# Pooled attention feeding a max-out MLP, one core: the last pair's x transposed on TensorE, a corrected model in the instruction planner, and a new rank between two kinds of jobs

## The chip, the cores and the metric

The kernel runs on one core of a Trainium2 chip. The metric is the device time of one execution, in microseconds (us), as the median of several executions. TensorE (PE in the profile) multiplies matrices into PSUM, ScalarE (ACT) does the exponentials, VectorE (DVE) moves results out of PSUM, GpSimd (POOL) casts inputs to bf16, and the queue of SyncE (SP) starts nearly all transfers. PEld is TensorE's loading of weights, which the profile lists on its own.

## The reference

Shapes: q, k, v are 8 batches x 8 heads x 1152 x 64; w1 and w2 are 512 x 1024; w_out is 1024 x 512.

```python
q_pool = q.reshape(B, H, S // 2, 2, D).mean(axis=3)      # 576 queries
attn = softmax(q_pool @ k.T / sqrt(D))
x = (attn @ v)  ->  [B * 576, H * D] = [4608, 512]
out = maximum(x @ w1, x @ w2) @ w_out
```

The kernel writes the maximum as `x @ w2 + relu(x @ (w1 - w2))`. With `wd = w1 - w2` and `w21 = w2 @ w_out`, the output is `x @ w21 + relu(x @ wd) @ w_out`.

## The kernel before

Two heads of a batch make a **pair**; there are 32 pairs, four to a batch. For each pair POOL casts q (adding the two pooled rows), k and v to bf16; q and k are brought into transposed form (`qpT`, `kT`), on TensorE for the first pairs and by a transposing DMA for the later ones. The scores of a pair form one long strip of 9 x 576 columns, cut into **groups** of 512 (324 in all). A group is two row tiles, one for each head: 64 rows of the array each, working at the same time (`scores`, L533). ACT takes the exponential of a group in one instruction (L540) into `et`. A group is written into one of three PSUM buffers `sps`, or of two after group `NARROW` (45), when the third is given to the other jobs.

All other TensorE work is a **job** of one kind, with its PSUM bank or banks and an evacuation:

- q and k: transposes for the next pairs (L410, L438).
- a: the product of `et` with `vE`, two jobs for a pair, each five chunks of nine matmuls (L384), then a reciprocal and a multiplication on DVE (L471, L473) into `xnat`.
- x: `xnat` of a pair transposed to `xT`, features by tokens. Batches 0 and 7 (`X_PE`) do this on TensorE in `xtrans_pe`: five transposes over the whole array (L589) into one bank and one DVE copy (L594). Batches 1 to 6 do it in `xtrans` by one transposing DMA for each pair (L575), issued by SP.
- w: the preparation of `w2T` and `w21`.
- h: a relu job, four matmuls over the features of up to 384 tokens with `wd`, evacuated through a relu into the ring `gT` (L686 on DVE, L682 on ACT in the tail). It needs `xT` of all four pairs of the batch.
- p: an output job of 128 tokens, four matmuls of `xT` with `w21` and eight of `gT` with `wo`, copied out (L715, L712) and stored (L662).

Full-array work is mode "f", work in two row tiles is mode "s". Between `NARROW` and the last group two h jobs or two p jobs run as a `Pair` in mode "s": a matmul of one job in the low rows beside one of the other in the high rows, in two banks.

**What sets the order.** No order is written by hand. The class `Plan` holds a model: a time at which each engine is free, a cost for each instruction, a latency after it, and one clock for all transfers, `dma_free`. `op` records an instruction at its modelled time. The loop at the end of the kernel asks at each step what TensorE could begin now by that model (a group of scores, or the next unit of a running job, by `rank`), and records it. `flush` issues loads, casts, transposing DMAs and stores when the model says that they are due; a load goes out only while `dma_free` is less than `DEPTH` = 4 us ahead. The recorded order is then emitted, with semaphores, as a fixed program for each engine. So each engine works through a fixed list: where an instruction's input is later than the model thought, all that stands behind it on its engine is late too.

`refill` gives free banks to jobs, in the order q, k, x, a, then w, p, h; a Pair needs two free banks, and no more than two Pairs run at a time (one while "a" jobs wait). Among running jobs `rank` decides: q and k 6, x 5, a 4, w 3, p 2, h 1.

Of the kernel before, what the change touches and what calls it, by code (L numbers as in the profile page):

```python
# [7 lines left out]
P = 128  # L8
# [7 lines left out]
class Plan:  # L16
# [11 lines left out]
    def __init__(self):  # L28
        self.ops = []
        self.writer = {}  # L30
        self.readers = {}
        self.free = {}
        self.dma_free = 0.0
        self.mode = None
        self.last = {}
        self.issued = 0
        self.pages = {}
# [19 lines left out]
    def fetch(self, t, n):  # L57
# [7 lines left out]
                t = max(t, self.pages[k])  # L65
        return t

    def op(self, eng, fn, r=(), w=(), dma=None, cost=0.1, mode="f", after=(), solo=False, done=None, n=0):
        me = len(self.ops)
        assert all(k in self.writer for k in r), r  # L70
        deps, raw = self.deps(r, w, after)
        if done is not None:
            deps.add(done)
        prev = self.last.get(eng)
        if prev is not None and (solo or self.ops[prev]["solo"]):
            deps.add(prev)
            raw.add(prev)
        self.last[eng] = me
        t = self.when(eng, r, w, after)
        if done is not None:  # L80
            t = max(t, self.ops[done]["seen"] + 0.05)
        if dma is not None:
            self.free[eng] = t + (1.3 if mode == "t" else 0.5)
            self.dma_free = max(self.free[eng] + 1.2, self.dma_free) + cost
            seen = self.dma_free + 0.7
        else:
            if eng == "PE" and mode != self.mode:
                t += 0.1
                self.mode = mode
            if eng == "PE":  # L90
                t = self.fetch(t, n)
            self.free[eng] = t + cost
            seen = t + cost + self.LAT[eng]
        self.ops.append(dict(eng=eng, fn=fn, deps=deps, raw=raw, dma=dma, w=tuple(w),
                             seen=seen, end=self.free[eng], solo=solo, done=done, mode=mode, cost=cost))
        for k in r:
            self.readers.setdefault(k, set()).add(me)
        for k in w:
            self.writer[k] = me
            self.readers[k] = set()  # L100
        return me
# [63 lines left out]
class Job:  # L165


    def __init__(self, kind, units, evac, done=None, nb=None, split=False):
        self.kind, self.units, self.evac, self.done = kind, units, evac, done
        self.nb, self.split = nb, split  # L170


# [16 lines left out]
class Pair:  # L189


    def __init__(self, one, two):
        self.kind, self.jobs = one.kind, (one, two)
# [12 lines left out]


def bass_funnel_attn__then__act_maxout2_kernel(
# [32 lines left out]
    with ctx:  # L241
# [138 lines left out]
        def plan_unit(u, ms, gate):  # L380

            def whole(e):
                for at, lhs, rhs, start, stop in u.parts:
                    last = e.matmul(fb[ms[0]][:, at:at + rhs.shape[-1]], lhs, rhs, start=start, stop=stop)  # L384
                return last

            def crossed(e):
                for p, q, phase, first, fin in u.parts:
                    for half, (at, lhs, rhs, *_), m in ((0, p, ms[phase]), (1, q, ms[1 - phase])):
                        last = e.matmul(fb[m][:, at:at + rhs.shape[-1]], lhs[rows(half)], rhs[rows(half)],  # L390
                                        start=first, stop=fin)
                return last

            if u.go is not None:
                fn = lambda e: u.go(e, ms[0])
# [5 lines left out]
        def dve(fn, r, w, cost):  # L401
            op("DVE", fn, r=r, w=w, cost=cost)

        def qtrans(i, lo=0, hi=QU, tag="", key=None):
            s = i % 2

            def go(e, m):
                mb = fb[m][:, :].bitcast(BF16)
                for u in range(lo, hi):
                    last = e.transpose(  # L410
                        mb[:, u * HP:(u + 1) * HP],
                        qp[s][:, u, :, :].rearrange("p h d -> p (h d)"), ident[0:HP, 0:HP])
                return last

            def evac(m):
                mb = fb[m][:, :].bitcast(BF16)
                dve(lambda e: e.tensor_copy(qpT[i % 3][:, lo * HP:hi * HP], mb[:, lo * HP:hi * HP]),
                    [f"f{m}"], [key or f"qpT{i % 3}", f"f{m}"] + (["qpT0.0"] if i == 3 else []),
                    0.06 + 0.038 * (hi - lo))
# [10 lines left out]
        def ktrans_pe(i, cuts=(0, 5, 9)):  # L430
# [3 lines left out]
            for lo, hi in zip(cuts, cuts[1:]):  # L434
# [8 lines left out]
                def evac(m, lo=lo, hi=hi):  # L443
                    mb = fb[m][:, :].bitcast(BF16)
                    dve(lambda e: e.tensor_copy(
                        kT[v3][:, lo:hi, :].rearrange("p t x -> p (t x)"),
                        mb[:, 0:(hi - lo) * P]),
                        [f"f{m}"], kkeys(i, lo, hi) + [f"f{m}"], 0.1 + (hi - lo) * 0.12)
# [133 lines left out]
        def xtrans_pe(i):  # L582
# [9 lines left out]
            def evac(m):  # L592
# [4 lines left out]
            return Job("x", [unit([f"xn{xs}.{2 * pr + half}" for half in range(2)] + ["ident"], 0.28, go)],  # L597
                       evac)

        def xkeys(n0, n1, cts):  # L600
            return [f"xT.{j}.{ct}" for j in range(n0 // HP, n1 // HP) for ct in cts]

# [8 lines left out]
        def w_cast(part, ct):  # L611
            if part == 0:
                dve(lambda e: e.tensor_copy(w2b[:, ct, :], w2f[:, ct, :]),
                    [f"w2f{ct}"], [f"w2b{ct}"], 0.6)
            elif part == 1:
                assert f"w2T{ct}" in plan.writer
                dve(lambda e: e.tensor_tensor(  # L617
                    wd[:, ct, :], w1f[:, ct, :], w2f[:, ct, :], ALU.subtract),
                    [f"w1f{ct}", f"w2f{ct}"], [f"wd{ct}", f"w2b{ct}", "w2f"], 1.2)
            else:  # L620
                dve(lambda e: e.tensor_copy(
                    wo[:, 2 * ct:2 * ct + 2, :], wof[:, 2 * ct:2 * ct + 2, :]),
                    [f"wof{ct}"], [f"wo{2 * ct}", f"wo{2 * ct + 1}"], 0.6)

        def w2t_job(ct):
            def go(e, m):
# [6 lines left out]
            def evac(m):  # L633
                mb = fb[m][:, :].bitcast(BF16)
                dve(lambda e: e.tensor_copy(
                    w2T[:, ct, :, :].rearrange("p f x -> p (f x)"), mb[:, 0:F]),
                    [f"f{m}"], [f"w2T{ct}", "w2T", f"f{m}"], 1.15)
            return Job("w", [unit([f"w2b{ct}", "ident"], 0.44, go)], evac)

        def w21_jobs():  # L640
# [178 lines left out]
        def flush():  # L819
# [22 lines left out]
                if plan.ops[plan.writer[f"osb{o}"]]["seen"] + 2.0 <= now():  # L842
                    store(*held.pop(o))
            for i in list(x_wait):
                if i // NHP in X_PE:
                    x_wait.remove(i)
                    queue["x"].append(xtrans_pe(i))
                elif plan.ops[plan.writer[f"xn{i // NHP % 2}.{2 * (i % NHP) + 1}"]]["seen"] <= now():
                    x_wait.remove(i)
                    xtrans(i)  # L850
# [54 lines left out]
        def refill():  # L905
# [2 lines left out]
            tail = nxt == NGR  # L908
            soon = now() + 0.05
            spare.sort(key=bank_at)  # L910
            pairs = sum(isinstance(r.job, Pair) for r in running)
            kinds = [r.job.kind for r in running]
            for kind in "qkxa" + ("wh" if queue["a"] and "p" in kinds else "wph"):
                while queue[kind] and spare and bank_at(spare[0]) <= now() + (9.0 if tail else 0.3):
                    wide = NARROW <= nxt < NGR and queue[kind][0].split
                    if wide and (len(spare) < 2 or pairs >= (1 if queue["a"] else 2)):
                        break
                    if wide and kind == "p" and "p" in kinds:
# [51 lines left out]
        def emit_unit(run):  # L970
# [4 lines left out]
                return  # L975
            running.remove(run)
            spare.extend(run.ms)
            for j, m in zip(job.jobs if isinstance(job, Pair) else (job,), run.ms):
                j.evac(m)
                finish(j)  # L980

        def finish(job):
# [58 lines left out]
        load("q", 4, load_q, "qraw1")  # L1041
        load("v", 3, load_v, "vraw0")
        start_w(1)
        rank = {"q": 6, "k": 6, "x": 5, "a": 4, "w": 3, "p": 2, "h": 1}
        while p_end[0] < NTOK:
            flush()
            refill()
# [91 lines left out]
```

## Time and profile before

| what | us |
|---|---|
| median of 3 executions | 384.81 (384.6 to 388.63) |
| the profiled execution, whole | 385.84 |
| its span, first to last instruction | 384.1 |
| PE busy | 362.5 (94%) |
| ACT busy | 316.9 (83%) |
| POOL busy | 162.1 (42%) |
| DVE busy | 140.6 (37%) |

The times of the table are of one profiled execution, apart from the first row. Busy time of PE is that of matmuls, which are pipelined and overlap, so a busy PE isn't one without gaps; the idle time before PEld shows gaps of some tenths of a microsecond that PE's row hides. In a row of the timeline stand the start, the duration, the engine, the line, the operation, what it writes and reads, the count, and in brackets the idle time before it with what ended it. A row of the groups has busy time and the mean of one in ns behind the bar.

### The profile page before, as it was taken

To read this page: it belongs to the slowest core of one execution; us is meant where nothing else is said; L and a number is where in the kernel's file an instruction comes from. 1 tells how busy PE (TensorE), PEld (TensorE's weight loads), DVE (VectorE), ACT (ScalarE), POOL (GpSimd) and SP (SyncE) were. 2 spreads that over 40 slices of the span, in tenths; PEclk is the share of its full clock that TensorE was granted. 3 is DMA by queue.
4 is the path that set the end of the run, shared out by engine and by line. 5 is a ranking of instruction groups with operands and counts; after the bars stand their busy time and mean duration, and the time that the engine had idled before them with its cause. 6 is when DMAs were issued, how large, how long until landed. Compare 5 with 4: busy or idle time off the path is not lost.

```text
span 384.1 us, 13179 instructions
## 1 busy us (share of the span) xinstructions
PE 362.5 (94%) x5928; PEld 232.9 (61%) x5936; DVE 140.6 (37%) x322; ACT 316.9 (83%) x358; POOL 162.1 (42%) x135
## 2 busy tenths in 40 slices
PE   4889989999599999999899999999999999999996
PEld 2456556666276666666575666666666666664754
DVE  3267943523132332512442413252324244351321
ACT  5998989899769999899889999999899998961320
POOL 2856587665433553634455365364454401000000
PEclk9898999999989999999999999999999999999999
DMA  8999999999997999999999899999999750203223
GB/s 281 409 390 401 361 270 318 223 340 294 266 343 228 212 268 234 272 255 241 277 262 239 267 264 285 229 272 267 248 274 205 129 111 6 56 3 82 58 55 82
DMA packets 95160, 89.09 MB, mean 232 GB/s; under 512 B 67456, under 2 KB 68224, under 8 KB 95104
## 3 DMA queue, kind: packets, MB, share of 16 engines
q1 hardware_dynamic: 94672, 87.86, 89.3%
q8 instruction: 46, 0.75, 0.8%
q10 hardware_dynamic: 432, 0.39, 0.4%
q14 instruction: 10, 0.08, 0.1%
HBM read 62.91 MB, written 9.44 MB: 188 GB/s over the span
## 4 chain that ended last, share of the span: by engine, by line
PE 79%; DMA 9%; ACT 6%; DVE 3%; SPq 1%; issue 1%; POOL 1%
PE sps L384 20%; PE sps L533 17%; PE fb L390 16%; PE fb L384 14%; PE sps L390 10%; ACT et L540 6%; DMA qraw<-in_q_dram 4%; DMA xT<-xnat 3%; DVE wd L617 1%; DMA kraw<-in_k_dram 1%; SPq L662 1%; POOL qp L353 1%; DVE xnat L473 1%; PE fb L589 0%; DVE stage L686 0%
## 5 line engine op out<-in xcount | busy, mean ns | idle before, releaser
L540 ACT ACTIVATE et<-sps 128x1024 bf16<-128x1024 f32 (+1 forms) x336 | 306.1, 1010 | 29.9 <-PE sps L533 27.7
L533 PE MATMUL sps<-qpT,kT 64*128 64x256 bf16 (+7 forms) x1162 | 121.4, 290 | 4.5 <-ACT et L540 2.8
L353 POOL TENSOR_TENSOR qp<-qraw 64x576 bf16<-64x576 f32 x62 | 87.7, 1414 | 14.1 <-DMA qraw<-in_q_dram 7.4
L367 POOL TENSOR_SCALAR vE<-vraw 128x1152 bf16<-128x1152 f32 x32 | 38.1, 1190 | 127.8 <-PE sps L384 84.4
L533 PEld LDWEIGHTS sps<-qpT,kT 64*128 64x128 bf16 x1162 | 46.9, 95 | 53.0 <-ACT et L540 26.9
L384 PEld LDWEIGHTS sps<-vE,et 128*128 128x128 bf16 x1530 | 49.3, 98 | 9.4 <-issue 4.4
L384 PE MATMUL sps<-vE,et 128*128 128x65 bf16 x1530 | 53.8, 194 | 0.0
L384 PEld LDWEIGHTS fb<-vE,et 128*128 128x128 bf16 x1350 | 43.7, 98 | 10.1 <-issue 4.1
L384 PE MATMUL fb<-vE,et 128*128 128x65 bf16 x1350 | 48.1, 194 | 0.8 <-DVE w L648 0.8
L329 POOL TENSOR_SCALAR kbf<-kraw 128x1152 bf16<-128x1152 f32 x31 | 36.4, 1173 | 13.4 <-DMA kraw<-in_k_dram 11.2
L686 DVE TENSOR_SCALAR stage<-sps 128x384 bf16<-128x384 f32 (+1 forms) x67 | 28.0, 452 | 36.6 <-PE sps L390 27.0
L390 PE MATMUL sps<-xT,wd 64*128 64x384 bf16 (+1 forms) x448 | 40.8, 286 | 0.2
L390 PE MATMUL fb<-xT,wd 64*128 64x384 bf16 (+1 forms) x384 | 35.0, 287 | 5.8 <-DMA xT<-xnat 5.4
L390 PE MATMUL fb<-wo,stage 64*128 64x512 bf16 x288 | 39.9, 376 | 0.0
L471 DVE RECIPROCAL rc<-sps 128x5 f32<-128x5 f32 x34 | 6.6, 195 | 65.8 <-PE sps L384 65.8
L686 DVE TENSOR_SCALAR stage<-fb 128x384 bf16<-128x384 f32 (+1 forms) x48 | 20.1, 461 | 24.0 <-PE fb L390 23.9
L390 PEld LDWEIGHTS fb<-xT,wd 64*128 64x128 bf16 x384 | 16.4, 94 | 15.5 <-DMA xT<-xnat 5.9
L390 PEld LDWEIGHTS sps<-xT,wd 64*128 64x128 bf16 x448 | 19.3, 94 | 9.9 <-DVE stage L715 0.6
L715 DVE COPY stage<-fb 128x512 f32<-128x512 f32 x19 | 12.3, 687 | 29.0 <-PE fb L390 24.4
L471 DVE RECIPROCAL rc<-fb 128x5 f32<-128x5 f32 x30 | 5.8, 195 | 42.3 <-PE fb L384 42.3
L390 PE MATMUL fb<-w,xT 64*128 64x512 bf16 x144 | 21.0, 376 | 0.1
L390 PEld LDWEIGHTS fb<-wo,stage 64*128 64x128 bf16 x288 | 13.4, 94 | 9.4
(59 smaller groups left out, 221.7 us busy)
## 6 DMA issues: line engine op xcount, KB each, us to landing
vraw<-in_v_dram SPq DMA_DIRECT2D x32, 576.0 KB, 7.1
kraw<-in_k_dram SPq DMA_DIRECT2D x31, 576.0 KB, 6.1
qraw<-in_q_dram SPq DMA_DIRECT2D x31, 576.0 KB, 5.2
out_dram<-stage SPq DMA_DIRECT2D x70, 128.0 KB, 3.9
xT<-in_moe_w_dram SPq DMA_DIRECT2D x4, 512.0 KB, 11.6
stage<-in_moe_w_out_dram SPq DMA_DIRECT2D x4, 512.0 KB, 15.1
stage<-in_moe_w_dram SPq DMA_DIRECT2D x4, 512.0 KB, 12.9
kT<-kbf SPq DMA_TRANSPOSE x27, 4.8
```

The costliest lines, as they stand in the source:

```text
L329: op("POOL", lambda g: g.tensor_scalar(kbf[s][:, :, :, :].rearrange("p t h d -> p h t d"), kraw[r][:, :, :, :], 1.0, 1.0, ALU.mult, ALU.mu ...
L353: op("POOL", lambda g, half=half, a=a: g.tensor_tensor(qp[s][:, :, half, :], a[:, :, 0, :], a[:, :, 1, :], ALU.add), r=[f"qraw{r}"], w=[f" ...
L367: op("POOL", lambda g: g.tensor_scalar(vE[r][:, :, :, 0:D].rearrange("p t h d -> p h t d"), vraw[r][:, :, :, :], 1.0, 1.0, ALU.mult, ALU.m ...
L384: last = e.matmul(fb[ms[0]][:, at:at + rhs.shape[-1]], lhs, rhs, start=start, stop=stop)
L390: last = e.matmul(fb[m][:, at:at + rhs.shape[-1]], lhs[rows(half)], rhs[rows(half)], start=first, stop=fin)
L471: dve(lambda e: e.reciprocal(rc[half][:, :], a[:, :, 64:65]), [f"f{m}"], [f"rc{half}"], 0.19)
L473: dve(lambda e: e.tensor_tensor(xnat[xs][:, i % NHP, :, half * D:half * D + D], a[:, :, 0:D], rc[half][:, :].unsqueeze(2).to_broadcast([P, ...
L533: last = e.matmul(sps[r][:, h, col:col + hi - lo], kT[i % 3][rows(h), t, :], qpT[i % 3][rows(h), lo:hi], start=True, stop=True)
L540: op("ACT", lambda e: e.activation(et2[:, :, c:c + z - a], sps[r][:, :, a - g * W:z - g * W], EXP, scale=scale), r=[f"s{r}"], w=keys + [f" ...
L617: dve(lambda e: e.tensor_tensor(wd[:, ct, :], w1f[:, ct, :], w2f[:, ct, :], ALU.subtract), [f"w1f{ct}", f"w2f{ct}"], [f"wd{ct}", f"w2b{ct} ...
L686: dve(lambda e: e.tensor_scalar_max(gT[:, ft, g0:g0 + size], fb[m][:, 0:size], 0.0), [f"f{m}"], w, 0.1 + size / 960.0)
L715: dve(lambda e: e.tensor_copy(osb[o][:, 0:n], fb[m][:, 0:n]), [f"f{m}"], [f"osb{o}", f"f{m}"], 0.1 + n / 966.0)
```

## The change

1. **x of the last pair of each batch.** In `flush`, pairs whose number within the batch is 3 go to TensorE in all batches, so those of batches 1 to 6 no longer use the transposing DMA. While `NARROW <= nxt < NGR` the new `xtrans_two` is used for every x job on TensorE: nine transposes of 64 rows by 128 columns, in the two row tiles (mode "s"), five of the low rows into one bank and four of the high rows into another, and three DVE copies in place of one. Such a job is `two`: it needs two banks and counts as a Pair.
2. **The planner's model.** SP and ACT are first free at 0.75 us; a plain transfer after a transposing one costs 0.65 more; a transfer is seen 0.8 us (a transposing one 1.2) after its end, where it was 0.7; several DVE costs change; VectorE's large casts of weights (mode "b") and POOL's work slow one another (`share`).
3. **Rank.** h has rank 2 and p has rank 1.

```diff
-        self.free = {}
+        self.free = {"SP": 0.75, "ACT": 0.75}
+        self.turned = False
...
+    def share(self, other, t, cost):
+
+        last = self.last.get(other)
+        if last is None or other == "DVE" and self.ops[last]["mode"] != "b":
+            return 0.0
+        both = 0.8 * max(0.0, min(cost, self.free[other] - t))
+        self.free[other] += both
+        self.ops[last]["seen"] += both
+        return both
...
             self.free[eng] = t + (1.3 if mode == "t" else 0.5)
+            if self.turned and mode != "t":
+                self.dma_free += 0.65
+            self.turned = mode == "t"
             self.dma_free = max(self.free[eng] + 1.2, self.dma_free) + cost
-            seen = self.dma_free + 0.7
+            seen = self.dma_free + (1.2 if mode == "t" else 0.8)
...
+            if eng == "POOL" or mode == "b":
+                cost += self.share("DVE" if eng == "POOL" else "POOL", t, cost)
...
-                    0.06 + 0.038 * (hi - lo))
+                    0.12 + 0.038 * (hi - lo))
...
-                        [f"f{m}"], kkeys(i, lo, hi) + [f"f{m}"], 0.1 + (hi - lo) * 0.12)
+                        [f"f{m}"], kkeys(i, lo, hi) + [f"f{m}"], 0.13 + (hi - lo) * 0.072)
...
+        def xtrans_two(i):
+            b, pr = i // NHP, i % NHP
+            xs, n0 = b % 2, b * SQ
+
+            def go(e, *ms):
+                for j in range(NCH + 1):
+                    for half, m in zip(range(2 if j < NCH else 1), ms):
+                        mb = fb[m][:, :].bitcast(BF16)
+                        last = e.transpose(mb[:, j * HP:(j + 1) * HP], xnat[xs][rows(half), pr, j, :],
+                                           ident[rows(half), rows(half)])
+                return last
+
+            def evac(*ms):
+                for half, m in enumerate(ms):
+                    n = NCH + 1 - half
+                    mb = fb[m][:, :].bitcast(BF16)[:, 0:n * HP].rearrange("p (j x) -> p j x", x=HP)
+                    to = xT[:, pr, n0 + half * HP:n0 + half * HP + NCH * P].rearrange(
+                        "p (j x) -> p j x", x=P)[:, :, 0:HP]
+                    parts = [(to, mb[:, 0:NCH, :], 0.3)]
+                    if half == 0:
+                        parts.append((xT[:, pr, n0 + NCH * P:n0 + SQ], mb[:, NCH, :], 0.13))
...
+            return Job("x", [unit([f"xn{xs}.{2 * pr + half}" for half in range(2)] + ["ident"],
+                                  0.19, go, "s")], evac, two=True)
...
-                    [f"w2f{ct}"], [f"w2b{ct}"], 0.6)
+                    [f"w2f{ct}"], [f"w2b{ct}"], 0.65, "b")
...
-                    [f"w1f{ct}", f"w2f{ct}"], [f"wd{ct}", f"w2b{ct}", "w2f"], 1.2)
+                    [f"w1f{ct}", f"w2f{ct}"], [f"wd{ct}", f"w2b{ct}", "w2f"], 1.2, "b")
...
-                    [f"f{m}"], [f"w2T{ct}", "w2T", f"f{m}"], 1.15)
+                    [f"f{m}"], [f"w2T{ct}", "w2T", f"f{m}"], 0.68)
...
-                if i // NHP in X_PE:
+                if i // NHP in X_PE or i % NHP == NHP - 1:
                     x_wait.remove(i)
-                    queue["x"].append(xtrans_pe(i))
+                    queue["x"].append((xtrans_two if NARROW <= nxt < NGR else xtrans_pe)(i))
...
-            pairs = sum(isinstance(r.job, Pair) for r in running)
+            pairs = sum(len(r.ms) > 1 for r in running)
...
-                    wide = NARROW <= nxt < NGR and queue[kind][0].split
+                    wide = queue[kind][0].two or NARROW <= nxt < NGR and queue[kind][0].split
...
-        rank = {"q": 6, "k": 6, "x": 5, "a": 4, "w": 3, "p": 2, "h": 1}
+        rank = {"q": 6, "k": 6, "x": 5, "a": 4, "w": 3, "p": 1, "h": 2}
```

More of the change, by code (lines that the diff above doesn't have):

```diff
@@ L165, with __init__ @@
 class Job:
-    def __init__(self, kind, units, evac, done=None, nb=None, split=False):
+    def __init__(self, kind, units, evac, done=None, nb=None, split=False, two=False):
         self.kind, self.units, self.evac, self.done = kind, units, evac, done
+        self.two = two
         self.nb, self.split = nb, split
@@ L192, in __init__ @@
     def __init__(self, one, two):
-        self.kind, self.jobs = one.kind, (one, two)
+        self.kind, self.jobs, self.two = one.kind, (one, two), False
         self.units = []
@@ L394, in plan_unit @@
             if u.go is not None:
-                fn = lambda e: u.go(e, ms[0])
+                fn = lambda e: u.go(e, *ms)
             else:
@@ L399, in plan_unit, with dve @@
                n=2 * len(ms) * len(u.parts) if u.parts else 2 * u.many)
-        def dve(fn, r, w, cost):
-            op("DVE", fn, r=r, w=w, cost=cost)
+        def dve(fn, r, w, cost, mode="f"):
+            op("DVE", fn, r=r, w=w, cost=cost, mode=mode)
         def qtrans(i, lo=0, hi=QU, tag="", key=None):
@@ L598, in xtrans_pe @@
                        evac)
+        def xtrans_two(i):
[17 more added lines that the diff above has]
+                        parts.append((xT[:, pr, n0 + NCH * P:n0 + SQ], mb[:, NCH, :], 0.13))
+                    for k, (to, a, cost) in enumerate(parts):
+                        op("DVE", lambda e, to=to, a=a: e.tensor_copy(to, a), r=[f"f{m}"],
+                           w=([f"xT.{(n0 + half * HP) // HP + 2 * j}.{pr}" for j in range(NCH)] if k == 0 else
+                              [f"xT.{(n0 + SQ) // HP - 1}.{pr}"]) + ([f"f{m}"] if k == len(parts) - 1 else []),
+                           after=under(n0, n0 + SQ) + [f"spill{pr}"], cost=cost)
+            return Job("x", [unit([f"xn{xs}.{2 * pr + half}" for half in range(2)] + ["ident"],
+                                  0.19, go, "s")], evac, two=True)
         def xkeys(n0, n1, cts):
@@ L622, in w_cast @@
                     wo[:, 2 * ct:2 * ct + 2, :], wof[:, 2 * ct:2 * ct + 2, :]),
-                    [f"wof{ct}"], [f"wo{2 * ct}", f"wo{2 * ct + 1}"], 0.6)
+                    [f"wof{ct}"], [f"wo{2 * ct}", f"wo{2 * ct + 1}"], 0.65, "b")
         def w2t_job(ct):
@@ L977, in emit_unit @@
             spare.extend(run.ms)
-            for j, m in zip(job.jobs if isinstance(job, Pair) else (job,), run.ms):
-                j.evac(m)
+            pair = isinstance(job, Pair)
+            for j, ms in zip(job.jobs, [[m] for m in run.ms]) if pair else [(job, run.ms)]:
+                j.evac(*ms)
                 finish(j)
```

## The prediction

> **What bounds the kernel now.** The page comes first, for the balance of the engines; then the table by stage; then the list of waits of TensorE; then the timeline around the two places that this list points to.
>
> ```profile
> span 384.1 us, 13179 instructions
> PE 362.5 (94%) x5928; PEld 232.9 (61%) x5936; DVE 140.6 (37%) x322; ACT 316.9 (83%) x358; POOL 162.1 (42%) x135
> ```
>
> TensorE is busy 94% of the span and ACT 83%. An average over stages says little, so here is the table by stage: the stretch and its length, then busy time (and instructions) of PE, PEld, DVE, ACT and POOL, then the granted clock, the share of the DMA engines and GB/s.
>
> ```profile
> 10.00:60.00 50.00, 44.77 (x714) 28.38 (x716) 28.44 (x51) 46.09 (x52) 34.68 (x26) 0.93 1.08 366
> 60.00:335.00 275.00, 267.81 (x4765) 173.92 (x4760) 95.19 (x234) 250.27 (x276) 125.03 (x99) 0.99 0.99 237
> 341.00:384.10 43.10, 39.60 (x324) 24.24 (x325) 10.58 (x23) 9.32 (x21) 0.00 (x0) 0.99 0.29 62
> ```
>
> From 60 to 335 us PE is idle for only 7.2 us of 275 and ACT for 24.7. After 341 us the scores are over, ACT is nearly done, and TensorE alone works for 43 us through relu and output jobs left over. So **the sum of TensorE's work and gaps sets the end**: a microsecond of TensorE won in the score stage lets relu and output work move out of the tail. What waits does PE have?
>
> ```profile
> PE fb L390 <- DMA xT<-xnat: 5.4, 2, 4.0
> PE fb L410 <- DVE qp L361: 4.8, 1, 4.8
> PE sps L533 <- ACT et L540: 2.8, 8, 0.6
> PE fb L410 <- POOL qp L353: 0.9, 1, 0.9
> PE fb L384 <- DVE w L648: 0.8, 1, 0.8
> ```
>
> The columns are total, times, longest. The 4.8 is one wait, for the cast of the first pair's q. The largest other item is two waits, of 4.0 and so 1.4 us, of relu jobs for x that a transposing DMA brings. The longer one:
>
> ```profile
> 95.16 3.14 SPq L662 DMA_DIRECT2D out_dram<-stage  x4
> 98.34 0.59 SPq L309 DMA_DIRECT2D qraw<-in_q_dram  x1
> 99.40 0.38 SPq L301 DMA_DIRECT2D kraw<-in_k_dram  x1
> 99.83 1.25 SPq L575 DMA_TRANSPOSE xT<-xnat  x1
> 105.91 0.82 PE L390 MATMUL fb<-xT,wd 64*128 64x192 bf16 x10 [4.02 <-DMA xT<-xnat]
> 107.00 1.02 ACT L540 ACTIVATE et<-sps 128x1024 bf16<-128x1024 f32 x1 [3.80 <-PE sps L533]
> ```
>
> The x of pair 7, the last of batch 1, stands on SP's queue behind four stores and two loads, is issued at 99.83 and lands some 6 us later. The planner had put relu matmuls that need it ahead of the next scores, so PE stops from 101.9 to 105.9, and ACT with it. The other wait is for the last pair of batch 3:
>
> ```profile
> 182.84 1.28 SPq L575 DMA_TRANSPOSE xT<-xnat  x1
> 190.19 0.26 PE L390 MATMUL fb<-xT,wd 64*128 64x192 bf16 x2 [1.43 <-DMA xT<-xnat]
> ```
>
> And the first gap is not over when it ends:
>
> ```profile
> 102.00:106.00 4.00, 0.09 (x2) 0.09 (x2) 0.72 (x2) 1.20 (x2) 0.00 (x0) 1.00 1.06 287
> 106.00:108.00 2.00, 1.94 (x37) 1.56 (x38) 0.62 (x2) 1.00 (x1) 0.00 (x0) 0.77 1.16 311
> 108.00:110.00 2.00, 2.00 (x32) 1.68 (x31) 0.51 (x2) 0.02 (x1) 0.00 (x0) 0.50 1.12 395
> 110.00:112.00 2.00, 2.00 (x51) 1.60 (x49) 0.22 (x2) 1.94 (x2) 0.00 (x0) 0.88 1.00 368
> 186.00:190.00 4.00, 2.69 (x52) 1.61 (x46) 1.87 (x6) 3.86 (x5) 1.29 (x2) 1.00 1.03 264
> ```
>
> After it the clock is 0.77, 0.50 and 0.88 in three stretches of 2 us, which loses 0.46 + 1.0 + 0.24 = **1.7 us**. After the short wait the clock stays at 1.00.
>
> **The change, part by part.** *The two waits go.* Both are for a last pair's x; the change takes all six such transposes off the DMA queue. Nothing on TensorE then waits for SP at a batch's end: -5.4 us of idle and -1.7 us of cold clock. What is late next is the product of the last pair itself, through DVE's normalisation, the transposes and DVE's copies, all of which the planner orders with durations it knows.
>
> *What TensorE takes on.* Nine transposes in 64 rows, six times. No row has them in two tiles; the nearest has nine in one tile, and the whole-array form has five:
>
> ```profile
> 12.68 0.33 PEld L410 LDWEIGHTS fb<-ident,qp 64*128 64x128 bf16 x9
> 337.75 0.38 PE L533 MATMUL sps<-qpT,kT 64*128 64x320 bf16 x4
> 338.06 0.28 PEld L589 LDWEIGHTS sps<-ident,xnat 128*128 128x128 bf16 x5 [0.21 <-issue]
> 338.44 0.11 PEld L390 LDWEIGHTS fb<-xT,wd 64*128 64x128 bf16 x4
> 338.55 0.46 DVE L594 COPY xT<-sps 128x576 bf16<-128x576 bf16 x1 [0.45 <-PE sps L589]
> ```
>
> The nine take 0.33 us in one tile. Two tiles at the same time could halve that to 0.17; at the pace of the whole-array form they would take 0.28 x 9 / 5 = 0.50. I take 0.33, the row of the same shape: 6 x 0.33 = **+2.0 us**, with 1.0 and 3.0 as ends.
>
> *Four transposes change form*: those of pair 3 and of the first three pairs of batch 7, which now are whole-array work between work in row tiles. In the fence above such a job costs 0.21 idle before, 0.28, and 0.10 to the next load (338.34 to 338.44): 0.59. In row tiles there is no change of mode: 0.33. So 4 x 0.26 = **-1.0 us**.
>
> *DVE.* Three copies of 256, 64 and 256 columns take the place of one of 576 (four times) or of none (six times).
>
> ```profile
> L594 DVE COPY xT<-fb 128x576 bf16<-128x576 bf16 x7 | 3.2, 456 | 1.6 <-PE fb L589 1.6
> L417 DVE COPY qpT<-fb 128x256 bf16<-128x256 bf16 x1 | 0.3, 291 | 0.5 <-PE fb L410 0.5
> ```
>
> At 0.29 for each of the large ones and at most that for the small one, 0.87 us a time; 10 x 0.87 - 4 x 0.46 = 6.9 us more on DVE, which from 60 to 335 us is busy for 95 of 275. Other evacuations have room around it, so I count nothing. Without that cover, the relu work of a batch would begin 0.4 us later, six times 0.4: 2.5 us.
>
> *SP and DMA.*
>
> ```profile
> xT<-xnat SPq DMA_TRANSPOSE x24, 6.0
> ```
>
> Six of these 24 issues, of 1.25 us each, leave SP's queue, and six transposes the DMA engines, whose share is 0.99 over the score stage. That can only bring other transfers forward; SP doesn't set the end, so nothing is counted.
>
> *The planner's model.* It computes nothing and adds no instruction; it re-orders. Three of the new costs can be set against rows:
>
> ```profile
> L445 DVE COPY kT<-fb 128x640 bf16<-128x640 bf16 x5 | 2.5, 492 | 5.7 <-PE fb L438 5.7
> L635 DVE COPY xT<-fb 128x1024 bf16<-128x1024 bf16 x4 | 2.7, 686 | 0.6 <-PE fb L629 0.4
> L617 DVE TENSOR_TENSOR wd<-stage,xT 128x1024 bf16<-128x1024 f32 x4 | 6.9, 1735 | 0.0
> ```
>
> The copy of five k blocks was modelled at 0.70 and is now at 0.49 (measured 0.492); that of `w2T` at 1.15, now 0.68 (0.686); the subtraction of weights at 1.2, now 1.2 plus what POOL costs it (1.735). So the model comes nearer to this trace. What that is worth can't be summed: the fixed order of some 13,000 instructions is drawn anew. Upper bound of the gain: PE's idle time between 10 and 60 us is 5.2 us, of which the rows above name 0.9 and 0.8 behind POOL and DVE. Upper bound of the loss: a wait like the present one, 5.7 us with its cold clock, at a new place. I take 0 and keep -3 and +6.
>
> *Rank.* Relu jobs go first among those running, and output jobs fill in. The work is the same; in the tail PE is busy 39.6 of 43.1 us in either order, about 3 us of the rest being the last copies and stores. I take 0.
>
> **The sum.** 385.84 (this execution) - 5.4 - 1.7 + 2.0 - 1.0 = 379.7 us. The profiled execution is 1.0 above the median of the runs shown (384.81), so by that median: **378.7 us**, 1.6% less. A change under 1% is about what a measurement of this kernel can't tell from none; that is 381.0 to 388.7.
>
> **Rivals.**
>
> *More is won* (0.08): the corrected model also closes gaps of 10 to 60 us, where the clock is 0.93 on the mean (3.5 us lost) and PE is idle for 5.2. Half of both is 4.3: 374.4. Against it: those gaps go with loads, k casts and ACT's pace, which the new numbers don't change.
>
> *The new order brings its own wait* (0.25): one gap of the present kind, 5.7 us, anywhere in the score stage, cancels the gain: 384.4. For it: the planner's order has 324 groups and over 100 jobs, and two misjudged transfers cost 7 us before; 18 transposing DMAs for x stay. Against it: those are for earlier pairs, which relu work doesn't need at once.
>
> *Banks* (0.10, slower). `xtrans_two` needs two banks and counts as a Pair, of which two may run. In the score stage four banks serve all jobs. An output Pair has now the lowest rank and keeps its two banks while relu Pairs pass; the x job then waits for a relu Pair to finish, its matmuls and two evacuations by L686:
>
> ```profile
> L686 DVE TENSOR_SCALAR stage<-fb 128x384 bf16<-128x384 f32 x26 | 13.3, 553 | 14.1 <-PE fb L390 14.1
> ```
>
> That is two times 0.55 plus about 0.9 us of matmuls, 2 us, and the "a" jobs queue for the same banks. If each of the ten x jobs delays the chain by 1 us on x and 0.2 on the product after it, 12 us come on top: 390.7. It decides from the point where PE has no other work ready while x waits; against it stands that a relu Pair or the output Pair itself is then there to run.
>
> *Loads are held back* (0.05, slower). Per pair the model's transfers sum to 8.5 us (k, q, v 4.45; transposes 3.15; stores 0.9); with 0.65 for one or two turns 9.2 to 9.8, close to the 10.4 us that a pair has (the scores end at about 341 us and begin at 7, for 32 pairs). With `DEPTH` a load then goes out later, casts and transposing DMAs follow, and ACT starves: 0.4 us a pair for 28 pairs, 389.9. It decides if the modelled sum passes the pair's time.
>
> *A cold clock from transposes* (0.02). The first two rows below show q transposes and behind them a clock of 0.57; if each of the six new jobs did that, at 1.7 us each, 378.7 + 10.2 = 388.9. Against it stands the x job on TensorE at 338.06 us, and the third row:
>
> ```profile
> 27.72 0.42 PE L410 MATMUL fb<-ident,qp 64*128 64x64 bf16 x9 [0.87 <-POOL qp L353]
> 28.00:32.00 4.00, 4.00 (x56) 2.70 (x54) 2.65 (x5) 3.30 (x4) 0.39 (x1) 0.57 1.05 398
> 336.00:344.00 8.00, 7.78 (x134) 4.93 (x132) 3.92 (x9) 6.51 (x8) 0.00 (x0) 1.00 0.01 2
> ```
>
> The clock is 1.00 around it. The Trainium skill, "TensorE: Matmul & The Clock Gate", section "Part 4: PE-mode transpose", says that transposes don't count as busy for the clock in the way that matmuls do, which speaks for this rival. By that rule the time would be its 388.9. With some 0.3 us of transposes among dense matmuls the trace doesn't bear it out.
>
> **How the numbers follow.** Forecast 0.50, with its own range 375.5 to 381.0 from the ends of the priced terms and a small loss or gain in the order; more won 0.08; own wait 0.25; banks 0.10, held loads 0.05 and cold clock 0.02 together 0.17. So faster 0.58, same 0.25, slower 0.17. The range from 374 to 389 leaves out about 0.05 below and 0.15 above.
>
> **What would show it.** Right: 18 DMA transposes of x; no wait of PE for x by DMA at a batch's end; clock 1.00 in every slice of the score stage; six more x jobs, of about 0.33 us of PEld, with no idle time before them from a change of mode; the tail shorter or the scores over earlier. Wrong: waits of PE or PEld for DVE's x copies, for banks, or for another DMA of several tenths at each batch; a new gap of microseconds; ACT waiting for scores for more than 27.7 us in all, the present sum:
>
> ```profile
> ACT et L540 <- PE sps L533: 27.7, 39, 3.8
> ```

## The result, and the profile after

The changed kernel takes 375.11 us (374.37 to 375.7), the kernel before beside it 386.01: a ratio of 0.971, 95% interval 0.965 to 0.977. The forecast was 378.7, within 374 to 389. The sign and the wide range held; the time lies 0.4 us below the forecast's own range, 375.5 to 381.0. The gain is 10.9 us where 6.1 were forecast, so nearly half of it has another source than the sum names. The profiled execution takes 375.68 us.

The page of the kernel after, its span and engines, and then the table by stage with the stretches that were read before (busy time and instructions of PE, PEld, DVE, ACT and POOL, then clock, DMA share, GB/s):

```profile
span 373.9 us, 13143 instructions
PE 358.2 (96%) x5910; PEld 231.7 (62%) x5910; DVE 142.6 (38%) x337; ACT 316.8 (85%) x361; POOL 163.7 (44%) x135
```

```profile
10.00:60.00 50.00, 46.90 (x789) 30.13 (x788) 28.86 (x56) 48.21 (x55) 36.22 (x26) 0.97 1.10 360
60.00:335.00 275.00, 271.09 (x4834) 176.36 (x4831) 100.59 (x250) 254.86 (x280) 125.35 (x99) 1.00 0.98 235
341.00:373.90 32.90, 29.82 (x190) 17.07 (x188) 6.05 (x13) 6.11 (x15) 0.00 (x0) 1.00 0.38 80
```

PE's idle time from 60 to 335 us falls from 7.2 to 3.9 us, its clock there is 1.00, and what is left after 341 us is 10.2 us shorter. The waits of PE and of ACT (total, times, longest), and the transposing transfers of x:

```profile
PE fb L427 <- DVE qp L378: 4.8, 1, 4.8
PE sps L550 <- ACT et L557: 2.7, 8, 0.6
PE sps L401 <- issue: 1.1, 2, 0.6
```

```profile
ACT et L557 <- PE sps L550: 18.1, 34, 1.0
```

```profile
xT<-xnat SPq DMA_TRANSPOSE x18, 6.3
```

No wait of PE for x by DMA is left, and ACT's wait for scores has gone from 27.7 to 18.1 us. The new x job, for the last pair of batch 1, in the timeline after:

```profile
92.93 0.49 DVE L490 TENSOR_TENSOR xnat<-sps,rc 128x320 bf16<-128x320 f32 x1
...
93.47 0.40 PEld L625 LDWEIGHTS sps<-ident,xnat 64*128 64x128 bf16 x9
93.69 0.30 PE L625 MATMUL sps<-ident,xnat 64*128 64x64 bf16 x9
94.03 0.58 DVE L639 COPY xT<-sps 128x256 bf16<-128x256 bf16 x3 [0.61 <-PE sps L625]
...
95.46 0.49 PE L407 MATMUL sps<-xT,wd 64*128 64x192 bf16 x8
```

DVE's normalisation ends at 93.42, the copies of x at 94.61, and the job's own loads of weights don't wait. Before, the same x was issued at 99.83 and landed at about 105.9.

*Where the time went.* ACT's busy time up to a moment is a measure of how far the scores have come. The same three stretches, first of the kernel before, then after:

```profile
0.00:60.00 60.00, 49.17 (x749) 30.95 (x754) 31.68 (x59) 51.38 (x57) 37.11 (x37) 0.94 1.03 352
60.00:110.00 50.00, 45.31 (x801) 29.96 (x797) 16.81 (x42) 41.20 (x45) 26.49 (x21) 0.97 1.15 291
110.00:320.00 210.00, 207.50 (x3706) 134.44 (x3704) 73.55 (x182) 195.34 (x216) 98.54 (x78) 1.00 1.01 239
```

```profile
0.00:60.00 60.00, 51.29 (x825) 32.63 (x826) 32.10 (x64) 53.48 (x60) 38.34 (x37) 0.97 1.06 347
60.00:110.00 50.00, 47.69 (x899) 32.41 (x896) 18.31 (x49) 45.58 (x51) 30.17 (x24) 1.00 1.09 275
110.00:320.00 210.00, 209.00 (x3653) 133.88 (x3651) 76.71 (x184) 197.94 (x219) 95.18 (x76) 1.00 1.01 239
```

After 60 us ACT is 2.1 us ahead, in the next 50 us it gains 4.4 more (the long wait was there), from 110 to 320 another 2.6. The last exponential of the scores and what follows it:

```profile
334.59 7.61 ACT L540 ACTIVATE et<-sps 128x1024 bf16<-128x1024 f32 x8 [0.47 <-PE sps L533]
```

```profile
327.26 4.70 ACT L557 ACTIVATE et<-sps 128x1024 bf16<-128x1024 f32 x5
```

These are before and after: the scores end at 342.2 and at 332.0. What comes behind them is 41.9 us long in both (384.1 - 342.2 and 373.9 - 332.0). So the whole gain of 10.2 us lies ahead of the last exponential, and **the tail did not grow** although the scores were done 10 us sooner.

### The profile page after: what moved, and what is told of

Read it like the earlier page. It is cut to its first block, busy times and chain, and to the rows that moved or that the text cites. A ratio compares the mean times of both kernels' runs of the same rounds, so it can differ in the third digit from the quotient of the medians.

```text
span 373.9 us, 13143 instructions
## 1 busy us (share of the span) xinstructions
PE 358.2 (96%) x5910; PEld 231.7 (62%) x5910; DVE 142.6 (38%) x337; ACT 316.8 (85%) x361; POOL 163.7 (44%) x135
## 4 chain that ended last, share of the span: by engine, by line
PE 78%; ACT 19%; DMA 1%; DVE 1%; issue 1%
PE sps L401 20%; ACT et L557 19%; PE sps L550 17%; PE fb L401 15%; PE fb L407 12%; PE sps L407 12%; DMA qraw<-in_q_dram 1%; DVE stage L761 0%; PE fb L455 0%; PE fb L427 0%; DVE kT L462 0%; DVE qp L378 0%; ACT stage L758 0%; PE sps L625 0%; PE fb L625 0%
## 5 line engine op out<-in xcount | busy, mean ns | idle before, releaser
L557 ACT ACTIVATE et<-sps 128x1024 bf16<-128x1024 f32 (+1 forms) x336 | 305.7, 1014 | 20.1 <-PE sps L550 18.1
L401 PEld LDWEIGHTS fb<-vE,et 128*128 128x128 bf16 x1485 | 47.6, 97 | 11.2 <-issue 4.8
L401 PE MATMUL fb<-vE,et 128*128 128x65 bf16 x1485 | 52.6, 193 | 0.0
L401 PEld LDWEIGHTS sps<-vE,et 128*128 128x128 bf16 x1395 | 44.2, 97 | 10.1 <-issue 5.3
L401 PE MATMUL sps<-vE,et 128*128 128x65 bf16 x1395 | 48.6, 193 | 1.1 <-issue 1.1
L732 DVE TENSOR_SCALAR stage<-sps 128x384 bf16<-128x384 f32 (+3 forms) x65 | 30.1, 496 | 50.6 <-PE sps L407 42.0
L407 PE MATMUL sps<-xT,wd 64*128 64x384 bf16 (+1 forms) x416 | 44.1, 313 | 0.0
L407 PE MATMUL fb<-xT,wd 64*128 64x384 bf16 (+1 forms) x288 | 28.6, 301 | 0.4 <-DVE stage L761 0.4
L732 DVE TENSOR_SCALAR stage<-fb 128x384 bf16<-128x384 f32 (+2 forms) x39 | 17.4, 484 | 27.8 <-PE fb L407 25.4
L407 PE MATMUL sps<-wo,stage 64*128 64x512 bf16 x160 | 23.4, 376 | 0.0
L490 DVE TENSOR_TENSOR xnat<-fb,rc 128x320 bf16<-128x320 f32 x33 | 16.2, 491 | 1.1
```

The costliest lines, as they stand in the source:

```text
L490: dve(lambda e: e.tensor_tensor(xnat[xs][:, i % NHP, :, half * D:half * D + D], a[:, :, 0:D], rc[half][:, :].unsqueeze(2).to_broadcast([P, ...
L557: op("ACT", lambda e: e.activation(et2[:, :, c:c + z - a], sps[r][:, :, a - g * W:z - g * W], EXP, scale=scale), r=[f"s{r}"], w=keys + [f" ...
L732: dve(lambda e: e.tensor_scalar_max(gT[:, ft, g0:g0 + size], fb[m][:, 0:size], 0.0), [f"f{m}"], w, 0.1 + size / 960.0)
```

## The experiments

The change has three parts: X (x of the last pairs), M (the planner's numbers), R (the rank). The six combinations other than the two kernels themselves were run, then variants. In the expectations, "exponential 48" is the start time of the 49th exponential, which the trace gives as 54.6 us before and 50.4 after.

**One part alone, and X taken out.**

```diff
 e1_x_only: before, with xtrans_two and
+                if i // NHP in X_PE or i % NHP == NHP - 1:
 e2_model_only: before, with the new costs, share, turned, seen and first free times
 e3_rank_only: before, with
+        rank = {"q": 6, "k": 6, "x": 5, "a": 4, "w": 3, "p": 1, "h": 2}
 e4_no_x: after, with
-                if i // NHP in X_PE or i % NHP == NHP - 1:
+                if i // NHP in X_PE:
```

> Only the x of each batch's last pair goes to TensorE, in two row tiles; the planner's numbers and the rank are those of before. Theory A (the two waits for x by DMA are most of the gain): the two waits of 4.0 and 1.4 us and the cold clock after the first go, the first 40 us stay as before, 378 to 380 us. Theory B (the corrected model is most of it): 383 to 386. Theory C (each edit draws a new order and the gains don't add): anywhere, with a new wait of 2 us or more of TensorE somewhere in the score stage.

> Only the planner's numbers are changed; x stays on the transposing DMA, the rank as before. Theory A: the first 60 us gain about 2 us (exponential 48 at 50.4 us in place of 54.6), one or two waits for x by DMA of 1 us or more stay, 382 to 385 us. Theory B: 377 or less. Theory C: anywhere.

> Only the ranks of relu and output jobs are exchanged. Theories A and B: within 1.5 us of before, 385 to 387, with the waits for x by DMA still there. A theory that the rank wins: 382 or less, with less idle time of ACT in the score stage. Theory C: anywhere, more than 2 us from before.

> The changed kernel with x back on the transposing DMA: model and rank new. Theory A: the waits for x by DMA come back, 380 to 384 us. Theory B: 375 to 377, as the changed kernel. Theory C: anywhere between 375 and 388.

| kernel | parts | median us (range) | ratio to before, 95% interval |
|---|---|---|---|
| e1_x_only | X | 380.63 (379.81 to 383.63) | 0.989 (0.984 to 0.995) |
| e2_model_only | M | 378.98 (378.37 to 379.94) | 0.983 (0.979 to 0.988) |
| e3_rank_only | R | 384.71 (382.86 to 386.52) | 0.998 (0.996 to 1.001) |
| e4_no_x | M, R | 377.47 (377.14 to 378.29) | 0.980 (0.976 to 0.984) |
| e5_no_rank | X, M | 380.04 (379.09 to 381.08) | 0.984 (0.978 to 0.991) |
| e6_no_model | X, R | 379.25 (379.01 to 379.49) | 0.982 (0.976 to 0.988) |
| after | X, M, R | 375.11 (374.37 to 375.7) | 0.971 (0.965 to 0.977) |

X alone brings 1.1%, M alone 1.7%, R alone nothing that can be measured. Theory A (X is most of it) and theory B (M is) both fall: either brings most of the same thing, and e4, which A put at 380 to 384 us with the waits back, takes 377.47 without them. Theory C holds in that the gains don't add; the new wait of 2 us or more that it names for e1 is in none of the six. But each kernel is one order drawn by the planner, and no run draws another order with the same parts, so a difference of 1 or 2 us between two kernels can be the draw rather than the part. In e1 and e2 alike PE has no wait for x by DMA. The kernel e2 still transposes pair 7's x by DMA, but in its order the transfer stands ahead of the stores. The SP queue and PE of e2 (M alone), then of e3 (R alone), where the wait is still there:

```profile
92.18 1.03 SPq L325 DMA_DIRECT2D qraw<-in_q_dram  x1
93.25 1.24 SPq L591 DMA_TRANSPOSE xT<-xnat  x1
...
102.87 4.35 SPq L678 DMA_DIRECT2D out_dram<-stage  x4
106.85 0.40 PE L406 MATMUL fb<-xT,wd 64*128 64x192 bf16 x5 [1.55 <-issue]
```

```profile
95.33 3.64 SPq L662 DMA_DIRECT2D out_dram<-stage  x4
99.43 0.40 SPq L301 DMA_DIRECT2D kraw<-in_k_dram  x1
99.89 0.49 SPq L322 DMA_DIRECT2D vraw<-in_v_dram  x1
100.43 1.25 SPq L575 DMA_TRANSPOSE xT<-xnat  x1
...
107.43 0.34 PE L390 MATMUL sps<-xT,wd 64*128 64x192 bf16 x2 [4.53 <-DMA xT<-xnat]
```

So the long wait can be removed in two ways, and its gain counts once: X and M together (0.984) are no better than M alone (0.983).

**The rank, the model and the form of the transposes taken out of the changed kernel, and one number of the model alone.**

```diff
 e5_no_rank: after, with
+        rank = {"q": 6, "k": 6, "x": 5, "a": 4, "w": 3, "p": 2, "h": 1}
 e6_no_model: after, with all costs and transfer numbers of before
 e7_x_whole: after, with
-                    queue["x"].append((xtrans_two if NARROW <= nxt < NGR else xtrans_pe)(i))
+                    queue["x"].append(xtrans_pe(i))
 e8_latency: before, with
+            seen = self.dma_free + (1.2 if mode == "t" else 0.7)
```

> The changed kernel with the ranks of before (output jobs ahead of relu jobs). Theories A and B: 375 to 376.5 us, the rank is worth nothing. If the rank matters: 378 or more, with a longer tail or more idle time of ACT in the score stage.

> The changed kernel with the planner's numbers of before. Theory A: 377.5 to 380 us, what is missing lies in the first 60 us (exponential 48 at about 54 us, a second cold spell of the clock). Theory B: 382 to 386.

> The changed kernel with the x of the last pairs transposed over the whole array (five transposes, one bank, one copy) in place of two row tiles. By the prediction's price of 0.26 us for each of ten jobs: 2.6 us slower, about 377.7 us. If the form doesn't matter: within 1 us of 375.1. If the two banks of the tiled form cost something: faster than 374.

> The kernel before with one number changed: a transposing transfer is seen 1.2 us after its end in the planner, in place of 0.7. If the two waits come from the planner's belief that x lands earlier than it does, half a microsecond moves little (the longer wait is 4.0 us): 384 to 387, a wait for x of 3 us or more stays. If any small edit draws an order without such waits: 380 or less.

Without the new rank the changed kernel takes 380.04 us, 4.9 more, though the rank alone brought nothing; added to X alone (e1 to e6) or to M alone (e2 to e4) it brings 1.4 and 1.5. Without the model 379.25: 4.1 more, as theory A said. That isn't a matter of cold spells of the clock at the start: one execution of e6 had the clock at 1.00 throughout and took 379.31. e7_x_whole takes 376.6 us (376.28 to 376.78; ratio 0.975, 0.967 to 0.982), 1.5 more than with row tiles where 2.6 was priced; the intervals of the two ratios overlap, and the order is another too, so the form is worth less than its price, and how much isn't separated. e8_latency takes 385.35 us (ratio 0.998, 0.994 to 1.001), as expected of a wait that is not a matter of half a microsecond: its profile still has a wait of 5.1 us for x.

*What does the rank do?* ACT's last rows of scores in e1 (X), e5 (X and M), each from its own timeline:

```profile
327.30 5.79 ACT L541 ACTIVATE et<-sps 128x1024 bf16<-128x1024 f32 x6
```

```profile
327.88 4.69 ACT L557 ACTIVATE et<-sps 128x1024 bf16<-128x1024 f32 x5
```

The scores end at 333.1 and 332.6, within 1.1 us of the changed kernel's 332.0. But their spans are 378.3 and 377.9: the tail is 45.2 and 45.3 us, in place of 41.9. So with the old rank the scores come out early all the same, and 3.4 us of relu and output work more is left over. The tails of the other kernels say the same, measured in the same way: with the rank 42.0 us (e3), 41.5 (e4) and 42.0 (e6), without it 43.6 (e2). In the kernel before it is 41.9, though its rank is the old one: its scores end 10 us later. TensorE's work behind 332 us, in e5 and then after:

```profile
332.00:390.00 58.00, 42.44 (x346) 25.55 (x345) 11.80 (x25) 9.96 (x22) 0.00 (x0) 1.00 0.22 46
```

```profile
332.00:390.00 58.00, 38.82 (x352) 25.66 (x351) 10.64 (x26) 8.48 (x22) 0.00 (x0) 0.98 0.26 55
```

To see which work takes longer ahead of it, the traces' matmuls can be grouped by kind, each counted from its own start to the next matmul's, beside what its columns need at 2.4 columns a nanosecond (two row tiles at half of that each). The rate is an assumption, the same for all kernels; output matmuls in row tiles fit it within 3% in the kernel before (72.2 us taken, 70.0 needed). Relu matmuls in row tiles, in us, with those that are 192 columns wide counted apart:

```
kernel         parts    taken   needed   over   narrow matmuls
before         -         64.3    51.2    13.1        384
e1_x_only      X         58.8    49.9     8.9        384
e2_model_only  M         59.6    51.2     8.4        384
e3_rank_only   R         61.2    51.2    10.0        384
e4_no_x        M, R      57.8    51.2     6.6        384
e5_no_rank     X, M      58.1    49.9     8.2        384
e6_no_model    X, R      57.3    51.2     6.1        256
after          X, M, R   53.7    51.2     2.5        128
```

Some of this is stops of 1 us or more that the profile lists: 5.4 us before (the two waits), 4.5 in e3, 1.6 in e2 and 1.1 in e6. Without them relu work lost 7 to 9 us in every kernel with the old rank. The new rank lowers the loss in each of the four pairs of kernels that differ in it alone: from 7.7 to 5.5 us (before, e3), from 6.8 to 6.6 (e2, e4), from 8.9 to 5.0 (e1, e6) and from 8.2 to 2.5 (e5, after). In the last two the number of narrow matmuls falls as well, in the first two it stays at 384. The code says how the two can hang together: `more_moe` starts a block of 192 tokens rather than 384 when neither an output job nor an "a" job is at hand. With output jobs last in rank, they can stay at hand; that they do so in e6 and after but not in e3 and e4 is seen only by the counts.

**The width of relu blocks, and half of the model.** Two theories for the rank were written down ahead of these runs: D, that it wins through fewer narrow blocks; E, that output work fills the gaps between relu Pairs.

```diff
 e9_no_rank_wide (on e5_no_rank) and e10_wide (on after):
-                if n1 - n0 < (min(most, LEAST) if idle or tail else HB - n0 % HB) or n1 == n0:
+                if n1 - n0 < (min(most, LEAST) if tail else HB - n0 % HB) or n1 == n0:
 e11_narrow: after, with
-        HB = RING // 3
+        HB = RING // 6
 e12_dve_model: after, with first free times, turned and seen of before
```

> The changed kernel with the ranks of before, and with relu blocks in the score stage only begun at their full width (384 tokens), where the planner would otherwise begin with 192 tokens when no output or product job is at hand. Theory D (the rank wins because output jobs stay at hand, so that fewer narrow relu blocks are begun): the time falls from 380.0 to 377 us or less. Theory E (the rank wins because output work fills the gaps between relu Pairs): 379 or more.

> The changed kernel with relu blocks in the score stage only begun at full width; 64 relu matmuls of 192 columns are left of 192. Theory D: as the changed kernel or up to 1 us faster, 374 to 375.5 us. If waiting for a full block leaves TensorE without work: 376.5 or more, with new waits for x.

> The changed kernel with all relu blocks of at most 192 tokens (HB = RING // 6), so 1312 relu matmuls of 192 columns in place of 192. Theory D, with some 14 ns lost for each narrow matmul as in the kernels with 384 of them: 1120 x 14 ns = 16 us more, 388 to 393. Theory E or any theory in which the width is of no account: 375 to 378.

> The changed kernel with the planner's numbers for transfers of before (first free times, turn, seen) and only those of VectorE and POOL corrected. If VectorE's and POOL's numbers win the first 60 us: exponential 48 at 50 to 51 us, 375 to 376.5. If the transfer numbers do: 54 us, 378 to 380, as with all numbers of before.

- e9_no_rank_wide: 383.78 us (382.6 to 385.25), 3.7 **slower** than with narrow blocks. Theory D in its plain form falls: width by itself is no gain. By the count above, relu matmuls lose 4.1 us in place of e5's 8.2, but the scores' matmuls lose 26.3 in place of 21.1.
- e10_wide: 379.67 us (379.42 to 380.62), 4.6 slower than after: 2.4 us lost by relu matmuls as in after's 2.5, but 23.5 by the scores in place of 19.2.
- e11_narrow: 387.21 us (386.38 to 389.1), 12.1 slower than after; 10.8 ns for each of the 1120 narrow matmuls that are more, three quarters of the 14 ns expected. Not all of it is the relu matmuls' own: in row tiles they lose 11.1 us in place of 2.5, and the scores' 23.0 in place of 19.2.
- e12_dve_model: 377.85 us (376.79 to 379.19), between the two expectations.

Why forced full width loses is seen from 82 to 98 us. The table by stage for after, then e5 (on which e9 is built), e9 and e10:

```profile
82.00:90.00 8.00, 8.00 (x151) 5.38 (x147) 2.60 (x6) 7.93 (x9) 5.57 (x5) 1.00 1.22 202
90.00:98.00 8.00, 7.30 (x131) 4.66 (x130) 2.58 (x9) 6.91 (x8) 5.06 (x4) 1.00 1.06 277
```

```profile
82.00:90.00 8.00, 7.64 (x143) 5.07 (x140) 3.62 (x11) 7.50 (x9) 5.08 (x4) 1.00 1.20 249
90.00:98.00 8.00, 7.62 (x124) 4.58 (x126) 1.49 (x6) 7.89 (x9) 5.15 (x5) 1.00 1.17 312
```

```profile
82.00:90.00 8.00, 5.12 (x72) 2.59 (x69) 1.43 (x3) 7.76 (x9) 5.06 (x4) 0.90 1.09 258
90.00:98.00 8.00, 6.68 (x107) 4.17 (x106) 1.96 (x7) 7.04 (x9) 5.06 (x4) 0.88 1.12 264
```

```profile
82.00:90.00 8.00, 5.56 (x61) 2.61 (x57) 1.93 (x4) 7.65 (x9) 5.05 (x4) 0.76 1.13 244
90.00:98.00 8.00, 6.68 (x107) 4.15 (x106) 1.96 (x7) 6.40 (x7) 5.07 (x4) 0.82 1.13 274
```

TensorE has too little to do while no full block is ready: from 82 to 90 us it is busy for 5.1 and 5.6 us of 8, in e9 with scores alone for most of it, each group waiting for ACT, and the clock falls. The new waits for x that were expected of e10 didn't come. In e9 the loads of score weights also wait longer for ACT than in e5, because no other work is ready (e5, then e9):

```profile
PEld sps L550 <- ACT et L557: 27.2, 90, 1.0
```

```profile
PEld sps L550 <- ACT et L557: 35.8, 99, 0.8
```

The scores end at 332.6 us in e9 and 333.0 in e10 all the same; what is lost shows as a tail of 48.7 and 45.9 us. So narrow blocks and TensorE standing without other work are both dear, and a relu block seems best full width **and** with output work at hand until it can begin. At e11's 10.8 ns, the 256 narrow matmuls that after has less than e5 would be 2.8 of the 4.9 us that the rank brings there, an estimate from above, since e11's loss isn't all the relu matmuls'. That the rest is output work between relu Pairs (theory E) fits e3, where relu work loses 2.2 us less at the same number of narrow matmuls, but no run isolates it. Why R brings nothing on the kernel before is not settled. One wait for x stays in e3, 4.5 us long, with a cold spell of 6.83 us behind it where before had 3.41. And no tail was seen below 41.5 us, so before, with 41.9, had none to shorten, as e1, e2 and e5 had.

In e12, ACT's 49th exponential starts at 50.6 us, as after, where e6, with all the old numbers, has 54.4. Part of the 3.8 us is e6's cold spell, 6.83 us long where e12 and after have 3.41. Without any cold spell ahead of it this exponential starts at 52.5 to 52.9 us with the old costs (e1, e3, e8) and at 50.2 to 50.3 with the new (e2, e5, e7). So **VectorE's and POOL's numbers win the first 60 us**, by some 2 us. What e12 lacks is the transfer numbers, and a wait for x by DMA is back, for the third pair of batch 2, not a last one:

```profile
138.92 0.50 PE L403 MATMUL fb<-xT,wd 64*128 64x384 bf16 x4 [1.96 <-DMA xT<-xnat]
```

No experiment beats the changed kernel.

## Why the prediction was right, and where it was short

- *The bound.* Right in what it says of the tail: a microsecond of TensorE won in the score stage shortens the end. Its row for the tail begins at 341 us, while the last exponential of the scores ends at 342.2. It missed that the scores end at 332 to 333 us in after, e1, e5, e9, e10 and e11 alike, though TensorE's idle time from 60 us to that end goes from 3.6 (e1) to 8.4 us (e11). Among these, the amount left for the tail tells the kernels apart. What holds the scores' end there wasn't tested; ACT is busy for 254.86 of the 275 us from 60 to 335.
- *The two waits, -5.4, and the cold clock, -1.7.* Right: both are gone, the clock is 1.00 from 60 us on, and ACT gains 4.4 us from 60 to 110. But X is not the only thing that removes them: M does too, and in e3 and e8, with x on the DMA, the shorter of the two is gone as well.
- *Six more transposes, +2.0.* Too dear: the ten jobs in row tiles take 2.1 us of TensorE between their first matmul and the next work, 0.21 each, so 1.3 for six. Eight of the ten take 0.12.
- *Four that change form, -1.0 by 0.26 each.* e7 gives 1.5 for all ten, 0.15 each, if all of its loss is the form's; between first matmul and next work its jobs take 0.39 each in place of 0.21.
- *DVE.* Right that it counts for nothing: no matmul and no load of weights is listed as waiting for the new copies. The size was too large: three copies take 0.58 us, not 0.87, and DVE is busy for 2.0 us more in all (142.6 for 140.6) where 6.9 were expected.
- *The planner's model, 0 between -3 and +6.* Too small in size: M is worth 4.1 us beside X and R (e6), beyond the end of 3, and 6.4 alone, where it also removes the long wait. "Half of both", the rival in which the corrected model closes early gaps, came true in part, and the argument against it (the new numbers don't change what those gaps go with) failed. ACT is 2.1 us ahead at 60 us, part of which is a cold spell that the profiled execution before had and others of the same order have not.
- *Rank, "I take 0".* **This step failed.** "The work is the same" is true of the matmuls and not of the time they take, and with X and M the rank is worth 4.9 us. The prediction judged it by the tail of the kernel before, 41.9 us behind the last exponential, where there was nothing to win; once the scores end 10 us sooner, the old rank leaves a tail of 45.3 (e5) and the new one 41.9. It had no row for the 7 to 9 us that relu matmuls lost in the score stage, because PE's busy time hides gaps of tenths; the new rank leaves 2.5 of it.
- *The sum.* That the time still came within 374 to 389 us is in part luck: two terms taken at 0 were worth several microseconds, both in the direction of the forecast.
- *X alone.* The sum of X's terms, -6.1, would be 379.2 from 385.34; e1 has 380.63. Of the 9.1 us by which its scores end sooner (342.2 to 333.1), 3.3 come back as a longer tail.
- *Rivals.* No new wait of microseconds and no cold clock from transposes appeared in the changed kernel, and no loss that would go with waits for banks or with loads held back: ACT waits for scores for 18.1 us in place of 27.7. That x of an earlier pair isn't needed at once does not hold in every order: e12 stands for 2.0 us for the third pair of batch 2.

## What to carry to other kernels

Where one list of instructions is drawn by a planner, price an edit by what becomes ready or stays at hand, not only by the instructions it adds: a rank that adds and removes no work was worth, beside the other parts, as much as the removal of the largest visible wait. Two parts that remove the same wait gain once, and a part that does nothing alone can be worth the most beside the others, so run the combinations. And where busy time is near 100%, count from one matmul's start to the next against what its columns need; the gaps stand there, not in the idle column.

## What the runs showed of the hardware

The clock at the start differs between executions of the same instructions. TensorE's first 1063 matmuls, up to about 75 us, stand in the same order in before and in e3_rank_only, yet over the first 60 us the clock is 0.94 in the one and 1.00 in the other, where ACT is 1.2 us further:

```profile
0.00:60.00 60.00, 48.84 (x775) 30.81 (x779) 31.01 (x60) 52.57 (x59) 36.62 (x37) 1.00 1.03 354
```

Each cold spell in these traces, but for those that begin in the last microseconds, is 3.41 us long at a clock of 0.5, or twice that: a loss of 1.7 or 3.4 us. The Trainium skill, "TensorE: Matmul & The Clock Gate", section "Part 1: The HAM clock gate (the "warmup" mystery)", gives a window of 3413 ns that runs freely, which these spells match; that the moment of the kernel's start against that window decides which execution has them is not shown here.

In e2, PE stands still for 1.55 us before 106.85 with nothing that the profile shows to release it, amid a chain of relu matmuls. Six stops of TensorE of 0.5 us or more behind 60 us that the profile puts down to "issue" stand in all the traces together: this one, 1.05 us in e6, 0.81 in e11, 0.64 in after, and 0.52 each in e3 and e4. Each of them ends 1.3 to 1.5 us after the end of a transfer of 16 KB on the queue that the page calls "q8 instruction" (46 of them in e2; the one here runs from 104.35 to 105.56 us). That suggests TensorE waiting there for its own next instructions, which the planner models in `fetch`. No run tests it, and two such stops ahead of 60 us (e5 at 55.0, e12 at 55.9) don't follow a transfer so closely.
